# Where eight small fills stand beside the first loads of the expert stage: one-core attention and expert layer

## The chip, the cores and the metric

The kernel runs on one core of one Trainium2 chip. The time is the device time of one execution in microseconds (us); lower is better. The core has five engines that run side by side: TensorE (PE, matrix products; its weight loads are listed as PEld), VectorE (DVE), ScalarE (ACT), GpSimd (POOL) and SyncE (SP, which here only issues DMAs). Each executes its own instructions in order and waits for others by semaphores. DMAs are issued by SP, ACT and POOL.

## The reference

Attention over 8 batches and 8 heads, with 32 global and 512 local positions of head size 64 (local positions see a window of 32 on either side and the global ones). Its output, 4352 rows of 512, goes through a layer of 8 experts, where each row goes to one:

```python
attn_out = _attn_ref(**attn_kwargs)
x = attn_out.transpose(0, 2, 1, 3).reshape(B * S, H * D)
...
expert_idx = np.argmax(logits, axis=1)          # logits: cosine of x and expert_emb, over tau
for e in range(E):
    mask = expert_idx == e
    h = np.maximum(x[mask] @ w1[e], 0.0)         # w1: 512 x 1024
    out[mask] = gate_w[mask, None] * (h @ w2[e]) # w2: 1024 x 512
```

## The kernel before

**Stage one, attention and routing.** For each batch the kernel computes the attention, chooses an expert for each row, and scatters the rows, 128 at a time, by indirect DMAs of POOL (line 838) to a table `xs` in DRAM. In `xs` each expert has a region of `CAP` rows that is filled from its start; a row holds 512 values, the gate and the row's number.

**The fills.** The last block of an expert's rows is seldom full. `fill_rest(e, eng)` (line 1119) writes 128 neutral rows from the tile `fill` behind the last row of expert `e`, at a place that it reads from `runi` (the running counts) by a register load. Expert 0's fill is issued by SP, those of experts 1 to 7 by POOL. Each is a DMA of 257 KB.

**Stage two, the items.** An item is a block of 128 rows of one expert. Two blocks of expert 0 (`EARLY = 2`) are computed early, between the last steps of stage one, by `early_block` (functions in the list `block`, products on line 196 of the profile). The items 0, 1, 2, ... follow. Where item `w` finds its rows and its weights stands in a small table `tab` (`table`, line 1127: some 45 tiny DVE operations, recorded in the list `listed`, and issued by `small`). The first 24 of them stand before the early blocks' last part, the others later. Items 0 and 1 need no table, as their places are known; SP, DVE, ACT and PE read the table by register loads from item 2 on.

One item, in `item` (line 1287):

- `load_x(w)`: four DMAs of 64 KB for the rows (`xr`, line 157) and a small one for the gate and number (`gt`, line 159), all on SP, in 512-byte pieces out of `xs`.
- `turn_x`, `split_x`: DVE turns the rows (`xk`, line 168), ACT and DVE make the two parts of each value, `xH` and `xL` (lines 1246 and 1247), since a product is formed as WH\*xH + WL\*xH + WH\*xL.
- `up(0)`, `up(1)`: 12 products on PE each (line 1315), one half of the hidden vector `h` each. `send_h` rectifies a half on ACT (`relu`, line 1264) and stores it to DRAM (`put_h`: `hd`, line 1272, a DMA of ACT's queue).
- `get_h(w, nh)`: SP loads the half back in a turned order (`hq`, line 1275); `turn_h`, `split_h` make `hk`, `hH`, `hL`.
- `down(0)`, `down(1)`: 12 products each; they stand one item later, between the next item's products (`pend["down"]`). `give` scales by the gate and scatters the rows to the output (POOL, line 176).
- `w_parts`, `slices`: the parts WH (ACT, lines 1210 and 1309) and WL (DVE, lines 1211 and 1310) of the next weights, from the staging tiles `stg`, which `first_w` and `load_w` load on SP.

**What sets the order.** All of this is written in program order per engine (`manual_schedule`): an engine's queue is the order of the calls. On SP, before item 0: the fill of expert 0, `load_x(0)`, `load_x(1)`, four loads of the second expert's first weights (`first_w(0, 0, 4)`, 512 KB each). In item 0: `load_x(2)`, `get_h(0, 0)`, a weight load, `get_h(0, 1)`, a weight load; in item 1: `load_x(3)` and so on. A load of rows by a register's value, as `load_x(2)`, must wait for every DMA that may have written the rows: all scatters and all fills. `load_x(0)` and `load_x(1)` wait for the scatters and expert 0's fill only.

Of the kernel before, what the change touches and what calls it, by code (L numbers as in the profile page):

```python
# [107 lines left out]
def tile_kernel(ctx: ExitStack, tc: tile.TileContext, qk, va, emb, tau, wraw, cst, out):  # L108
    nc = tc.nc
# [160 lines left out]
    with ExitStack() as actx:  # L270
# [41 lines left out]
        ahead = [0]  # L312
# [44 lines left out]
        first = io.tile([P, 4, RS], F32, name="raw")  # L357
# [16 lines left out]
        for n, i in enumerate((0, NBQ - 2)):  # L374
            for q in range(4):
                m = _mask_of(i + q % 2) * P
                rows = slice(32 * q, 32 * q + 32)
# [615 lines left out]
        for g in loads:  # L993
            n = len(loads[g])
# [121 lines left out]

    fills = []

    def fill_rest(e, eng):

        r = eng.value_load(runi[:1, e : e + 1], min_val=e * CAP, max_val=e * CAP + NT)
        ins = eng.dma_start(xs[ds(r, P), :], fill)
        for f in fills + scat + early:
            tc.declare_no_dep(ins.ins, f.ins, reason="disjoint rows")
        fills.append(ins)
# [77 lines left out]
        return tab, nitem  # L1203

    tab = {}

    def first_parts(hf, c):

# [4 lines left out]
    first = [(0, c) for c in (0, 2, 4, 6, 1, 3, 5, 7)] + [(1, c) for c in range(8)]  # L1213

    def slices(n):
        for _ in range(n):
            first_parts(*first.pop(0))
# [10 lines left out]
    def load_x(w):  # L1228
        r = entry(nc.sync, 0, w, NE * CAP)
        return rows_of(xrs[w % 2], gts[w % 5], xs[ds(r, P), :], True)  # L1230

    def load_w(w):
        r = entry(nc.sync, 1, w, 2 * NE - 1)
        src = wraw[ds(r, 1), :, :].rearrange("a p (c n) -> p (a c) n", n=WRUN)
        for n in range(2):
            cs = slice(2 * n, 2 * n + 2)
            new = {"cond": entry(nc.sync, 4 + n, w, 1)}
            nc.sync.dma_start(st0[w % 2][:, cs, :WRUN], src[:, cs, :], **new)
# [13 lines left out]
    def turn_x(w):  # L1252
        turn_blocks(xk, xrs[w % 2])

    def split_x(w):
        parts_of(flat(xHs[w % 2]), flat(xLs[w % 2]), xk)
# [20 lines left out]
    def turn_h(nh):  # L1277
        turn_blocks(hk, hqs[nh])
# [8 lines left out]
    def item(w, pend):  # L1287

        xH, xL = xHs[w % 2], xLs[w % 2]
        rp = entry(nc.tensor, 2, w, 1)  # L1290
        regs = entries(w)
        if w < 2:
            held.append((w, regs))
        reads = []
        made = []
        todo = [(w, regs, c) for c in range(8)]
        if w == 0:
            todo = todo[:4]
        elif w == 1:
            todo = [(*held[0], c) for c in range(4, 8)] + [(*held[1], c) for c in range(4)]  # L1300
        elif w == 2:
            todo = [(*held[1], c) for c in range(4, 8)] + todo

        def w_parts(n):
            for _ in range(min(n, len(todo))):
                v, (ra, rv), c = todo.pop(0)
                cs = slice(c * 512, (c + 1) * 512)
                s3 = cols(st0[v % 2], cs.start, cs.stop).unsqueeze(1)
                a = nc.scalar.copy(WH[c][:, ds(ra, 1)], s3)  # L1309
                b = nc.vector.tensor_tensor(WL[c][:, ds(rv, 1)], s3, WH[c][:, ds(rv, 1)], ALU.subtract)  # L1310
                made.extend([(v, c, a), (v, c, b)])

        def product(o, a, W, hf, start=False, stop=False):
            w3 = W[:, ds(rp, 1), hf * 512 : (hf + 1) * 512]
            return nc.tensor.matmul(o.unsqueeze(1), a, w3, start=start, stop=stop)  # L1315

        def up(nh):
            g = ps_1.tile([P, 512], F32, name="g1")
            for k in range(4):
                c = 2 * k + nh  # L1320
                reads.append(product(g, xH[:, k, :], WH2[c], 0, start=k == 0))
                reads.append(product(g, xH[:, k, :], WL2[c], 0))
                reads.append(product(g, xL[:, k, :], WH2[c], 0, stop=k == 3))
            return g

        out = {}

        def down(nh):
            if nh == 0:
                out["g2"] = g2s[w % 2]  # L1330
            g, ks, made = out["g2"], range(4 * nh, 4 * nh + 4), []
            for k in ks:
                made.append(product(g, hH[:, k, :], WH2[k], 1, start=k == 0))
                made.append(product(g, hH[:, k, :], WL2[k], 1))
            for k in ks:
                made.append(product(g, hL[:, k, :], WH2[k], 1, stop=k == 7))
            return made

        def done():
            give(gts[w % 5], out["g2"], obp.tile([P, DM + 1], F32, name="ob"))  # L1340

        def send_h(nh, g):
            relu(nh, g)
            put_h(w, nh)

        ga = up(0)
        if "done" in pend:
            pend["done"]()
        if w > 2 and w + 1 < NI:
            load_w(w + 1)  # L1350
        if w + 2 < NI:
            load_x(w + 2)
        if w == 0:
            send_h(0, ga)
            slices(3)
            send_h(1, up(1))
            slices(3)
            block[9]()
            block[10]()
            get_h(w, 0)  # L1360
            first_w(1, 0, 1)
            get_h(w, 1)
            first_w(1, 1, 2)
            w_parts(4)
        elif w == 1:
            send_h(0, ga)
            w_parts(2)
            turn_h(0)
            split_h(0)
            gb = up(1)  # L1370
            reads.extend(pend["down"](0))
            send_h(1, gb)
            first_w(1, 2, 3)
            get_h(w, 0)
            first_w(1, 3, 4)
            w_parts(2)
            load_w(w + 1)
            turn_h(1)
            split_h(1)
            turn_x(w + 1)  # L1380
            split_x(w + 1)
            w_parts(4)
            get_h(w, 1)
            reads.extend(pend["down"](1))
        elif w == 2:
            turn_x(w + 1)
            turn_h(0)
            split_x(w + 1)
            split_h(0)
            turn_h(1)  # L1390
            send_h(0, ga)
            w_parts(2)
            split_h(1)
            gb = up(1)
            reads.extend(pend["down"](0))
            send_h(1, gb)
            w_parts(2)
            get_h(w, 0)
            load_w(w + 1)
            w_parts(8)  # L1400
            get_h(w, 1)
            reads.extend(pend["down"](1))
        else:
            if w < NI - 1:
                turn_x(w + 1)
            turn_h(0)
            if w < NI - 1:
                split_x(w + 1)
            w_parts(1)
            split_h(0)  # L1410
            turn_h(1)
            send_h(0, ga)
            w_parts(1)
            split_h(1)
            w_parts(1)
            gb = up(1)
            reads.extend(pend["down"](0))
            send_h(1, gb)
            get_h(w, 0)
            w_parts(8)  # L1420
            get_h(w, 1)
            if w in (8, NSURE - 1):
                nc.gpsimd.drain()
            reads.extend(pend["down"](1))
        for v, c, m in made:
            for r in reads:
                tc.declare_no_dep(m.ins, r.ins, reason="the other slot")
                tc.declare_no_dep(r.ins, m.ins, reason="the other slot")
        for i, (v, c, m) in enumerate(made):
            for u, d, o in last_made + made[:i]:  # L1430
                if c == d and (v - u) % 2:
                    tc.declare_no_dep(m.ins, o.ins, reason="another half")
        last_made[:] = made
        after = {"down": down, "next": done}
        if "next" in pend:
            after["done"] = pend["next"]
        return after
# [12 lines left out]
    with tc.manual_schedule():  # L1450
        nc.vector.tensor_copy(runi, run[:1])
        fill_rest(0, nc.sync)
        load_x(0)
        load_x(1)
        for e in range(1, NE):
            fill_rest(e, nc.gpsimd)
        listed = []
        tab["tab"], nitem = table(listed)

        def small(n):  # L1460
            while listed and n:
                listed.pop(0)()
                n -= 1

        small(24)
        for i, f in enumerate(block[:9]):
            if i:
                f()
            slices((4, 0, 2, 0, 2, 0, 0, 0, 0)[i])
            if i == 8:  # L1470
                first_w(0, 0, 4)
                turn_x(0)
                split_x(0)
                small(len(listed))
                slices(2)
                turn_x(1)
                split_x(1)
        pend = {}
        for w in range(NSURE):
            pend = item(w, pend)  # L1480
# [94 lines left out]
```

## Time and profile before

| what | value |
|---|---|
| runs shown | 699.07 us median of 3 (695.35 to 699.75) |
| profiled execution | 692.65 us |
| its span, first to last instruction | 690.9 us |
| mean granted TensorE clock | 0.977 of full speed |
| PE busy | 635.1 us, 92% of the span |
| fills of POOL | 7, of 257.0 KB each |

The profiled execution is 6.4 us faster than the median of the runs shown; 1.75 us of its time lie outside the span. Times inside the trace count from the span's start. Attention and routing end at about 265 us, and the items run from 270 us to the end.

### The profile page before, as it was taken

Reading aid. Unit: us, or ns where it says so; the run is one execution under the profiler, and the core shown is the slowest. Engines: PE = TensorE matmul, PEld = TensorE weight load, DVE = VectorE, ACT = ScalarE, POOL = GpSimd, SP = SyncE. Lnnn points to the kernel's source line nnn. Section 1 sums busy time; section 2 is a strip of 40 time slices with the busy share of each in tenths; the row PEclk is TensorE's granted clock in tenths of the full one; section 3 lists DMA queues with packets and bytes.
Section 4 is the critical chain, followed back from the end, with each engine's and each line's share of the span. In section 5 each row is a group of like instructions: output and inputs, shape, how many; then the busy total and the mean of one; then the engine's idle time right before and its main releaser. Section 6 shows DMA issues by size and latency. Waiting matters only on the chain.

```text
span 690.9 us, 23126 instructions
## 1 busy us (share of the span) xinstructions
PE 635.1 (92%) x7423; PEld 495.4 (72%) x7425; DVE 525.5 (76%) x1724; ACT 455.6 (66%) x962; POOL 98.6 (14%) x179
## 2 busy tenths in 40 slices
PE   8889888779788897898999999999999999999994
PEld 4667666667576644577888888887787877878883
DVE  2859778698777875797888887887787877878881
ACT  4667758658676433676777677775676757677771
POOL 2011122212213341001011011010101010101101
PEclk9999999999989999999999999999999999999997
DMA  8998889788899538877565587678877779685551
GB/s 271 304 277 249 259 265 280 216 272 285 271 302 279 170 138 259 238 251 221 164 168 150 154 242 206 206 217 263 228 229 229 210 255 261 195 267 162 148 156 36
DMA packets 125207, 154.67 MB, mean 224 GB/s; under 512 B 15945, under 2 KB 81609, under 8 KB 125080
## 3 DMA queue, kind: packets, MB, share of 16 engines
q1 hardware_dynamic: 80744, 114.48, 57.1%
q10 hardware_dynamic: 38016, 18.88, 9.1%
q0 software_dynamic: 6320, 19.71, 7.5%
q8 instruction: 69, 1.13, 0.7%
q14 instruction: 58, 0.48, 0.2%
HBM read 161.36 MB, written 40.94 MB: 293 GB/s over the span
## 4 chain that ended last, share of the span: by engine, by line
PE 52%; DMA 14%; DVE 12%; issue 12%; ACT 6%; SPq 3%; ACTq 1%; DVEq 1%; POOL 0%; POOLq 0%; another core or an unknown queue 0%
PE g L1315 26%; PE po L196 8%; PE pt L199 7%; PE pt L196 5%; PE s_ps L196 5%; DMA xr<-xs 4%; DVE WL L1310 4%; DMA hq<-hd 3%; DMA hd<-h 3%; ACT WH L1309 3%; DVE hk L168 2%; DMA raw<-in_qk_dram 2%; PE g L196 1%; SPq L157 1%; ACT h L1264 1%
## 5 line engine op out<-in xcount | busy, mean ns | idle before, releaser
L1310 DVE TENSOR_TENSOR WL<-stg,WH 128x512 f32 (+1 forms) x288 | 184.4, 683 | 34.3 <-ACT WH L1309 33.6
L1309 ACT CAST WH<-stg 128x512 f32 (+1 forms) x288 | 163.6, 618 | 37.0 <-ACT h L1264 35.5
L1315 PE MATMUL g<-WH,hH 128*128 (+1 forms) x288 | 114.7, 398 | 11.3 <-ACT hH L1246 11.1
L1315 PE MATMUL g<-WH,xH 128*128 (+1 forms) x288 | 113.1, 393 | 3.5 <-ACT xH L1246 3.5
L1315 PE MATMUL g<-WL,hH 128*128 (+1 forms) x288 | 113.4, 394 | 0.0
L1315 PE MATMUL g<-WL,xH 128*128 (+1 forms) x288 | 112.9, 392 | 0.5 <-DVE WL L1310 0.5
L1315 PE MATMUL g<-WH,xL 128*128 (+1 forms) x288 | 113.0, 392 | 0.0
L176 POOL DMA_INDIRECT out_dram<-ob x37 | 36.0, 974 | 387.6 <-DVE xk L168 186.7
L553 ACT ACTIVATE pb<-pb,nm 128x128 f32<-128x128 f32 x256 | 80.0, 395 | 10.3 <-DVE nm L536 10.3
L1315 PE MATMUL g<-WH,hL 128*128 (+1 forms) x288 | 77.9, 393 | 0.0
L1315 PEld LDWEIGHTS g<-WH,hH 128*128 128x128 f32 x288 | 54.9, 190 | 27.6 <-ACT hH L1246 12.3
L168 DVE STREAM_TRANSPOSE hk<-hq 128x512 f32<-128x512 f32 x72 | 50.6, 703 | 24.8 <-DMA hq<-hd 21.1
L1315 PEld LDWEIGHTS g<-WH,xH 128*128 128x128 f32 x288 | 54.5, 189 | 15.8 <-ACT xH L1246 4.3
L1315 PEld LDWEIGHTS g<-WL,xH 128*128 128x128 f32 x288 | 54.3, 189 | 13.0 <-DVE WL L1310 1.5
L1315 PEld LDWEIGHTS g<-WH,hL 128*128 128x128 f32 x288 | 54.6, 190 | 11.5
L1315 PEld LDWEIGHTS g<-WL,hH 128*128 128x128 f32 x288 | 54.8, 190 | 11.2
L1315 PEld LDWEIGHTS g<-WH,xL 128*128 128x128 f32 x288 | 54.5, 189 | 11.6 <-DVE xL L1247 0.4
L1246 ACT CAST hH<-hk 128x512 fp32r<-128x512 f32 x72 | 44.6, 620 | 25.4 <-DVE hk L168 24.8
L196 PE MATMUL s_ps<-raw 64*32 64x128 f32 (+1 forms) x1792 | 46.8, 281 | 11.8 <-issue 10.8
L536 DVE CUSTOM_DVE_ANT_0 pb<-s_ps,mask 128x128 f32<-128x128 f32 x192 | 44.2, 285 | 15.5 <-PE s_ps L196 15.5
L196 PE MATMUL po<-vt,pT 128*32 128x65 f32 x2048 | 46.4, 231 | 10.3 <-issue 10.0
L565 ACT COPY pT<-pt 128x512 f32<-128x512 f32 x64 | 34.6, 588 | 31.7 <-PE pt L199 30.3
(197 smaller groups left out, 880.6 us busy)
## 6 DMA issues: line engine op xcount, KB each, us to landing
stg<-in_wraw_dram SPq DMA_DIRECT2D x70, 1024.0 KB
vt<-in_va_dram SPq DMA_DIRECT2D x96, 260.0 KB
hd<-h ACTq DMA_DIRECT2D x72, 256.0 KB
hq<-hd SPq DMA_DIRECT2D x72, 256.0 KB
raw<-in_qk_dram SPq DMA_DIRECT2D x56, 304.0 KB
xr<-xs SPq DMA_DIRECT2D x152, 64.0 KB
vt<-in_va_dram SPq DMA_DIRECT2D x32, 130.0 KB
stg<-in_wraw_dram SPq DMA_DIRECT2D x16, 256.0 KB
```

The costliest lines, as they stand in the source:

```text
L157: made.append(nc.sync.dma_start(x[32 * g : 32 * g + 32].rearrange("p (t n) -> p t n", n=P), src))
L168: nc.vector.transpose(xT.rearrange("p (k t n) -> p t k n", k=4, t=4), x.rearrange("p (t k n) -> p t k n", t=4, k=4))
L176: nc.gpsimd.indirect_dma_start(out=out[:, :], out_offset=bass.IndirectOffsetOnAxis(ap=ob[:, DM : DM + 1].bitcast(U32), axis=0), in_=ob[:, ...
L196: return counted(nc.tensor.matmul(out, lhsT, rhs, start=start, stop=stop), 4 if lhsT.dtype == F32 else 2)
L199: return counted(nc.tensor.transpose(out, in_, eye), 2)
L536: nc.vector.tensor_tensor_reduce(state["pb", g][grp][:, cs], ps[:, grp, cs], mk, -ISQ, 3.0e38, ALU.add, ALU.min, nm[:, n : n + 1],)
L553: nc.scalar.activation(pb[:, cs], pb[:, cs], AF.Exp, bias=nm[:, n : n + 1], scale=-1.0)
L565: nc.scalar.copy(pT, state["tp", g, grp])
L1246: nc.scalar.copy(tH, x)
L1309: a = nc.scalar.copy(WH[c][:, ds(ra, 1)], s3)
L1310: b = nc.vector.tensor_tensor(WL[c][:, ds(rv, 1)], s3, WH[c][:, ds(rv, 1)], ALU.subtract)
L1315: return nc.tensor.matmul(o.unsqueeze(1), a, w3, start=start, stop=stop)
```

## The change

The seven fills on POOL get a wait: each may start only when the ten DMAs of `load_x(0)` and `load_x(1)` have landed. In item 0 the first half of `h` is rectified and stored (`send_h(0, ga)`) first; `turn_x(1)`, `split_x(1)` and the rest of the table, which stood before item 0, follow it, and two of six `slices` move from before the second half's store to behind it.

```diff
-    def fill_rest(e, eng):
+    def fill_rest(e, eng, behind=()):
 
         r = eng.value_load(runi[:1, e : e + 1], min_val=e * CAP, max_val=e * CAP + NT)
         ins = eng.dma_start(xs[ds(r, P), :], fill)
+        for o in behind:
+            tc.add_manual_dep(
+                ins.ins,
+                o.ins.name,
+                mybir.DependencyInfo(mybir.DependencyClass.Sync, mybir.DependencyReason.DATA),
+                reason="the first rows go ahead",
+            )
...
             load_w(w + 1)
+        if w == 0:
+            send_h(0, ga)
+            turn_x(1)
+            split_x(1)
+            small(len(listed))
         if w + 2 < NI:
             load_x(w + 2)
         if w == 0:
-            send_h(0, ga)
-            slices(3)
+            slices(2)
             send_h(1, up(1))
-            slices(3)
+            slices(4)
...
         fill_rest(0, nc.sync)
-        load_x(0)
-        load_x(1)
+        rows = load_x(0) + load_x(1)
         for e in range(1, NE):
-            fill_rest(e, nc.gpsimd)
+            fill_rest(e, nc.gpsimd, rows)
...
                 turn_x(0)
                 split_x(0)
-                small(len(listed))
                 slices(2)
-                turn_x(1)
-                split_x(1)
```

How the queues stand. On POOL, from the last scatter of rows on; `mask` is the output of the first early block, `DMAHW` are semaphores of DMAs of SP and ACT, `DMASW` of POOL's. Before:

```order
L1121 TENSOR_LOAD runi_74 [waits DVE_49]
L1121 ISA x2
L1122 ISA
L1122 DMA xs_57<-fill_80 128x514 [waits DMASW2_49]
L1121 TENSOR_LOAD runi_74
L1121 ISA x2
L1122 ISA
L1122 DMA xs_57<-fill_80 128x514 [waits DMASW3_49]
L176 DMA out_0_dram<-mask_134 4352x512 [waits DMASW4_49,DVE_49,Activation_49]
```

On POOL, the same place with the change:

```order
L1121 TENSOR_LOAD runi_74 [waits DVE_49]
L1121 ISA x2
L176 DMA out_0_dram<-mask_134 4352x512 [waits DMASW2_49,DVE_49,Activation_49]
L1122 ISA
L1122 DMA xs_57<-fill_80 128x514 [waits DMAHW4_49,DMAHW3_49,DMAHW5_49,DMAHW2_49,DMAHW6_49,DMAHW1_49,DMAHW7_49,DMAHW0_49,DMASW3_49]
L1121 TENSOR_LOAD runi_74
L1121 ISA x2
L1122 ISA
L1122 DMA xs_57<-fill_80 128x514 [waits DMASW4_49]
```

The output of the early block now stands ahead of all fills, and the first fill waits for the loads; the other six follow it in the queue, each behind its own register load.

On SP, `load_x(2)` and what is queued behind it, with the change; the DMASW semaphores of its first DMA are those of the seven fills:

```order
L1239 TENSOR_LOAD tab_5894 [waits DVE_49]
L1239 ISA x2
L1487 TENSOR_LOAD nitem_5895 [waits DVE_49]
L1487 ISA x2
L157 ISA
L157 DMA xr0_5768<-xs_57 32x4x128 [waits DMASW5_49,DMASW4_49,DMASW6_49,DMASW3_49,DMASW7_49,DMASW1_49,DMAHW5_49,DMASW0_49,DVE_49]
L157 ISA
L157 DMA xr0_5768<-xs_57 32x4x128 [waits DMAHW6_49]
```

On SP, the same place before, up to the first load of `h`:

```order
L1226 TENSOR_LOAD tab_5894 [waits DVE_49]
L1226 ISA x2
L157 ISA
L157 DMA xr0_5768<-xs_57 32x4x128 [waits DMASW5_49,DMASW3_49,DMASW6_49,DMASW2_49,DMASW7_49,DMASW1_49,DMAHW4_49,DMASW0_49,DVE_49]
L157 ISA
L157 DMA xr0_5768<-xs_57 32x4x128 [waits DMAHW5_49]
L157 ISA
L157 DMA xr0_5768<-xs_57 32x4x128 [waits DMAHW6_49]
L157 ISA
L157 DMA xr0_5768<-xs_57 32x4x128 [waits DMAHW7_49]
L159 ISA
L159 DMA gt2_5772<-xs_57 128x1x2 [waits DMAHW1_49]
```

SP's order of DMAs is unchanged; a register load of `nitem` (the number of items), which stood far behind, now stands ahead of `load_x(2)`. The wait for the seven fills is there before and after.

On ACT, item 0 before (`xH1` is item 1's, `h` the first half, `hd00` its store):

```order
L1246 CAST xH1_5782<-xk_5775 128x512 [waits DVE_49]
L1264 ACTIVATE h_5787<-g1_6001 128x4x4x32 [waits PE_49,Activation_49]
L1272 DMA hd00_58<-h_5787 128x4x128 [waits DMAHW3_49,Activation_49]
L1210 CAST WH2_5754<-stg1_91 128x512
L1210 CAST WH3_5755<-stg1_91 128x512
```

With the change, its lines' numbers larger by 13, ACT has:

```order
L1277 ACTIVATE h_5787<-g1_5975 128x4x4x32 [waits PE_49,Activation_49]
L1285 DMA hd00_58<-h_5787 128x4x128 [waits DMAHW2_49,Activation_49]
L1259 CAST xH1_5782<-xk_5775 128x512 [waits DVE_49]
L1223 CAST WH2_5754<-stg1_91 128x512
L1223 CAST WH3_5755<-stg1_91 128x512
```

The first half's rectifier and store have moved ahead of item 1's `xH`. PE's order is the same in both.

## Rows read from the trace of the kernel before

**Rows 1.** Page, part 4: share of the span by engine on the chain that ended last.

```profile
PE 52%; DMA 14%; DVE 12%; issue 12%; ACT 6%; SPq 3%; ACTq 1%; DVEq 1%; POOL 0%; POOLq 0%; another core or an unknown queue 0%
```

**Rows 2.** Waits of PE, 260 to 330 us: us in total, times, longest.

```profile
PE g L1315 <- ACT hH L1246: 5.4, 3, 2.3
PE g L1315 <- ACT xH L1246: 3.5, 1, 3.5
```

**Rows 3.** Chain that ended last, 260 to 270 us: start, duration, what.

```profile
262.72 5.24 DMA xr<-xs
...
269.79 0.50 PE g L1315
```

**Rows 4.** DMA queues, 263 to 268 us: packets, MB, share of 16 engines.

```profile
q1 hardware_dynamic: 1163, 0.47, 49.2%
q0 software_dynamic: 220, 0.70, 39.1%
```

**Rows 5.** Chain, other stretches: loads of `xr` and `hq`, issue to landing.

```profile
320.07 4.43 DMA hq<-hd
...
495.35 3.99 DMA xr<-xs
...
598.02 2.57 DMA hq<-hd
```

**Rows 6.** Stretches: length, busy of PE, PEld, DVE, ACT, POOL, granted clock, DMA share, GB/s.

```profile
265.00:270.00 5.00, 1.53 (x5) 0.46 (x4) 0.94 (x2) 1.16 (x3) 0.00 (x0) 1.00 0.84 209
270.00:275.00 5.00, 5.00 (x15) 3.68 (x15) 4.52 (x26) 0.78 (x2) 0.00 (x0) 0.66 0.90 333
...
285.00:290.00 5.00, 2.70 (x12) 1.91 (x11) 2.93 (x5) 2.86 (x6) 0.00 (x0) 1.00 1.05 265
```

**Rows 7.** Timeline of PE, 264 to 296 us: start, duration, instruction, idle before.

```profile
288.52 0.50 PE L1315 MATMUL g<-WH,hH 128*128 128x512 f32 x1 [2.30 <-ACT hH L1246]
...
292.67 0.50 PE L1315 MATMUL g<-WH,hH 128*128 128x512 f32 x1 [1.10 <-ACT hH L1246]
```

**Rows 8.** Timeline of POOL, 250 to 300 us.

```profile
256.86 1.17 POOL L1122 DMA_DIRECT2D xs<-fill  x2
...
262.22 0.54 POOL L1122 DMA_DIRECT2D xs<-fill  x1 [0.90 <-issue]
263.63 0.54 POOL L1122 DMA_DIRECT2D xs<-fill  x1 [0.87 <-issue]
283.40 1.01 POOL L176 DMA_INDIRECT out_dram<-ob  x1 [19.23 <-ACT WH L1309]
```

**Rows 9.** DMA issues, 245 to 300 us: count, KB each, median us to landing.

```profile
xs<-fill POOLq DMA_DIRECT2D x7, 257.0 KB, 4.8
```

**Rows 10.** Timeline of SP, 251 to 300 us.

```profile
266.55 0.57 SPq L159 DMA_DIRECT2D gt<-xs  x1
...
275.52 2.15 SPq L157 DMA_DIRECT2D xr<-xs  x4
277.86 0.66 SPq L159 DMA_DIRECT2D gt<-xs  x1
279.66 0.36 SPq L1275 DMA_DIRECT2D hq<-hd  x1
```

**Rows 11.** Timeline of ACT and DVE in items 0 and 1.

```profile
273.74 0.17 DVE L1134 CAST tab<-tabf 128x6 int32<-128x6 f32 x1
...
276.33 0.59 ACT L1264 ACTIVATE h<-g 128x512 f32<-128x512 f32 x1
...
287.11 0.70 DVE L168 STREAM_TRANSPOSE hk<-hq 128x512 f32<-128x512 f32 x1
...
293.26 0.70 DVE L168 STREAM_TRANSPOSE xk<-xr 128x512 f32<-128x512 f32 x1
```

**Rows 12.** DMA queue of SP, 268 to 275 us: packets, MB, share of 16 engines.

```profile
q1 hardware_dynamic: 801, 2.07, 87.3%
```

More of the change, by code (lines that the diff above doesn't have):

```diff
@@ L1205, in tile_kernel, with small @@
     tab = {}
+    listed = []
+    def small(n):
+        while listed and n:
+            listed.pop(0)()
+            n -= 1
     def first_parts(hf, c):
@@ L1452, in tile_kernel @@
         fill_rest(0, nc.sync)
-        load_x(0)
-        load_x(1)
+        rows = load_x(0) + load_x(1)
         for e in range(1, NE):
-            fill_rest(e, nc.gpsimd)
-        listed = []
+            fill_rest(e, nc.gpsimd, rows)
         tab["tab"], nitem = table(listed)
[L1460 to L1463, printed above, removed]
         small(24)
```

## The prediction, made before the changed kernel was run

> **What bounds the kernel now.** I read first the chain that ended last, by engine, to see whether one engine is the limit. PE holds 52% of it, DMAs 14%, DVE 12% and ACT 6% [rows 1]: over most of the kernel PE is the limit, and the other shares come from places where PE waits. The change touches one of these, so I read PE's waits from 260 to 330 us. There are few: one of 3.5 us for item 0's `xH`, and three for `hH`, 5.4 us together [rows 2]. At the first, the chain shows why: the last load of item 0's x goes out at 262.72, takes 5.24 us and lands at 267.96, and PE starts item 0 at 269.79, 1.83 us after that [rows 3]. While that load is under way, two queues share the DMA engines: SP's with 49.2% and POOL's with 39.1% of their time, and POOL's 0.70 MB are fills [rows 4]. Elsewhere a load of `xr` has taken 3.99 us, and one of `hq` 2.57 [rows 5]. After the wait PE's granted clock is 0.66 of full speed from 270 to 275 us [rows 6], between its two levels of 1.2 and 2.4 GHz; in those 5.00 us it loses 5.00 x 0.34 = 1.7 us against full speed.
>
> The next place is the first `down(0)`. PE ends item 1's products at 288.52 - 2.30 = 286.22, waits 2.30 us for `hH`, and 1.10 more ahead of `down(1)` at 292.67 [rows 7]. So what PE gains early only counts if `down(0)` of item 0, at 288.52, comes earlier too. This decides the case: what comes ahead of `down(0)` on the other engines must gain as well.
>
> **The change part by part.**
>
> *Item 0's x without the fills.* The fills no longer go out ahead of x0. Its landing then lies between 5.24 us (nothing gained: its own 512-byte pieces set it) and 2.57 us, the quickest load out of DRAM in [rows 5]. I take 2.57, since the one thing known to share those microseconds, POOL's queue, is gone. x0 lands at 262.72 + 2.57 = 265.3, PE starts at 265.3 + 1.83 = 267.1, and gains 2.7 us. The wait ahead of it shrinks from 3.5 to 0.8 us, and with so short a wait I expect no fall of the clock: the wait of 2.30 us ahead of 288.52 left it at 1.00 from 285 to 290 us [rows 6, 7]. That gives the 1.7 us as well: 4.4 us together. Item 1's products would end at 286.22 - 4.4 = 281.8.
>
> *The fills.* POOL now waits for the last of the ten loads, item 1's gate and number, issued at 266.55 [rows 10]. With 2.57 us, the first fill can go at 269.1. The other six stand behind it, each with its register load in between. Fills that were not held up went out 263.63 - 262.22 = 1.41 us apart; two in a row with their registers ready take 1.17 us, or 0.59 each [rows 8]. I take 1.41, as the order shows a register load ahead of each fill: the last one goes out at 269.1 + 6 x 1.41 = 277.6 (by 0.59, 272.6). A fill took 4.8 us to land [rows 9], with x0 and x1 beside it. Now it has four weight loads, 2.07 MB at 87.3% of the engines [rows 12], beside it, so I keep 4.8: the last lands at 282.4, or at 277.4 by the quicker pitch. Behind the fills on POOL stands the output of the second early block, at 283.40 [rows 8], which comes after 277.6 + 0.5 anyway. The early block's first output goes out a little earlier, and no one reads it.
>
> A rule of the Trainium skill speaks for an earlier landing. Its page "DMA: Bandwidth & Descriptors" (section "Anatomy of one DMA — SWDGE (gpsimd) path") gives a DMA of POOL a fixed part of some 2.0 us and then 436 GB/s: 2.6 us for 257 KB, an estimate by that page against the row's 4.8. By it the last fill would land at 280.2 and the sum below would be -0.7 in place of +1.5, or 698.4. The page's figure is for one DMA alone, which the row is not, so the row stays.
>
> *What waits for the fills.* SP's first DMA of `load_x(2)` waits for all seven; it did so before as well, but then they had landed long before 275.52, where the table let it go (its last operation ends at 273.91 [rows 10, 11]). Now the table comes later: it stands behind item 0's first half on DVE. By how much I bound from rows: relu0 was at 276.33 [rows 11] and would be some 4 us earlier with item 0, the table's rest ran up to 273.91 with DVE busy 4.52 of 5 us [rows 6], so it ends at about 276 and SP's register loads, one more of them (`nitem`), at about 278. That is earlier than 282.4 and costs nothing while the fills are later; by the quicker pitch it costs up to 1 us.
> So `load_x(2)` goes at 282.4 in place of 275.52. On SP everything behind it waits: its own five DMAs (275.52 to 278.52, 3.0 us [rows 10]), then `get_h(0, 0)`, a weight load, `get_h(0, 1)`. `get_h(0, 0)` went at 279.66 and now goes at 285.4. Between 2.57 and 4.43 us [rows 5] for its landing I take 2.57, as the fills are then done: 288.0. From DVE's turn of `hk` at 287.11 to PE at 288.52 are 1.41 us [rows 7, 11], so `down(0)` starts at 289.4: 0.9 us later than before. The stores of `h` go ahead 4 us, and gain nothing, for SP is not there to read them.
>
> *PE's wait moved.* PE now waits from 281.8 to 289.4, 7.6 us in one piece where it had 2.30. The wait of 3.5 us was followed by a clock of 0.66, so I expect the same loss, 1.7 us, over `down(0)` and what follows; 1.10 of it lie where PE waited ahead of `down(1)` anyway. Cost: 0.6 us, between 0 (the wait of 2.30 cost nothing) and 1.7.
>
> *The rest.* Item 2's x lands some 7 us later, at about 285.4, and DVE turns it at 293.26 [rows 11]. The `slices` moved behind the second half run on ACT and DVE beside PE's long wait. `xH` of item 1 stands behind relu0 on ACT, but PE reads it only after item 0's second half. All three at nothing; their cover is PE's work on item 0 and the wait ahead of `down(0)`.
>
> *Sum.* -4.4 early, given back whole; +0.9 for `down(0)`, +0.6 for the clock: +1.5 us. The profiled execution's 692.65 would be 694.15. It lies 6.4 us under the median, and the same difference on the median is 699.07 + 1.5 = 700.6.
>
> **The rivals.**
>
> *The early gain survives.* If the fills go 0.59 us apart, they have landed at 277.4, `get_h(0, 0)` goes at 280.4 and lands at 283.0, `down(0)` starts at 284.4, 4.1 us earlier, after a wait of 2.6 us like that of before, without loss of clock: 695.0. For it speaks that registers could be loaded while the first fill waits, and that the page's landing is shorter; against it that only the first fill's registers stand ahead of the wait. At most the 1.10 us ahead of `down(1)` go as well: 693.9.
>
> *The fills land later still: slower.* Each us by which the last fill lands after 280.9 makes the kernel a us slower, for PE's whole wait there hangs on it. Fills of 7 x 0.257 = 1.80 MB and weights of 2.07 MB now want the engines together. At 209 GB/s, the rate of 265 to 270 us with the same kinds of traffic [rows 6], 3.87 MB from 267.1 on take 18.5 us, to 285.6: 3.2 us beyond my 282.4, so +4.7, or 703.8. For it: 87.3% of the engines are taken by weights until 275 us. Against it: at 333 GB/s [rows 6] the same is done at 278.7. The skill's same page, section "Issuing engines are not separate DMA queues", says that queues of different issuers share the 16 engines, and the drawn-out x0 of [rows 3, 4] agrees.
>
> *It does not do what it says.* If x0's 5.24 us come of its small pieces, or of x1's loads behind it, item 0 starts at 269.8 as before, the clock falls as before, item 1's products end at 286.2 and only a wait of 3 us stands ahead of `down(0)`. Then -4.4 and +0.6 drop out, +0.9 stays, and a later x1 adds up to its own lateness, some 1 us: 700 to 701, near my number by another way.
>
> **How the numbers follow.** My forecast, 700.6 with a range of its own of 699 to 702.5: 0.50. The gain survives, 695.0: 0.26. The fills land later, 703.8: 0.16. It does not do what it says, 700.5: 0.08. The range reaches from 694.0, the end of the gain, to 704.5: it leaves out the later half of the third case and a part of the second, and runs that scatter as before's (695.35 to 699.75). About 1%, 7 us, is what a measurement of this kernel can tell from no change, so faster begins under 692.1, which not even the second case reaches, and slower over 706.1, which the third reaches only if the last fill lands after 287: 0.05 each.
>
> **What would show it.** In the changed profile: x0's last load lands in under 4 us, PE's wait for `xH` is under 1.5 us and the clock of 270 to 275 is 1.00 (first step); POOL's fills begin at about 269 and end at about 278, 1.4 us apart (second); SP's `load_x(2)` goes at about 282, its wait put down to a fill, and `get_h(0, 0)` right behind it, not behind the store (third); PE's largest wait of the stage is that ahead of the first `down(0)`, some 7 us, with a clock under 0.8 in the 5 us behind it (fourth). The prediction is wrong if the last fill lands before 280 or after 284, or if what follows `down(0)` soaks up its shift: the third wait for `hH` is 5.4 - 2.30 - 1.10 = 2.0 us long [rows 2], and a later start could shorten it.

## The result, and the profile after

The changed kernel takes 700.83 us (median of 20 runs, 694.89 to 706.22), the kernel before 696.22 us on the same chip (20 runs, 686.41 to 709.88): a ratio of 1.0127 with a 95% interval of 1.0091 to 1.0163. The ratio compares the fast runs of each kernel, while the medians of all runs lie 4.6 us, or 0.7%, apart, and the profiled executions of e2, f3 and g1 further down are among their kernels' slow runs. The forecast of 700.6 was near the measured time, but that was luck: it stood for a step of 1.5 us from 699.07, the median of three runs, and the twenty have a median 2.85 us under that. The step itself is three times the forecast's by the medians (4.6 us), and six times by the ratio (1.27% of 699 us are 8.9). The profiled execution takes 699.77 us with a span of 698.1.

The places where the time goes are read from the changed kernel's trace in the order of [rows 2 to 12]. PE's waits from 260 to 330 us first (us in total, times, longest):

```profile
PE g L1328 <- ACT hH L1259: 12.3, 2, 8.2
```

The wait for `xH` of [rows 2] is gone, and the waits for `hH` have grown from 5.4 to 12.3 us. The timeline of PE puts one ahead of the first `down(0)` and one ahead of the second half of item 1's `h`:

```profile
289.28 0.79 PE L1328 MATMUL g<-WH,hH 128*128 128x512 f32 x1 [8.15 <-ACT hH L1259]
...
309.06 0.50 PE L1328 MATMUL g<-WH,hH 128*128 128x512 f32 x1 [4.20 <-ACT hH L1259]
```

The stretches (columns as in [rows 6]) show the gain in front, and the price behind it:

```profile
270.00:275.00 5.00, 5.00 (x17) 3.01 (x16) 3.29 (x21) 4.10 (x9) 1.86 (x4) 1.00 1.01 349
275.00:280.00 5.00, 5.00 (x22) 3.92 (x21) 4.93 (x13) 3.21 (x6) 0.60 (x2) 1.00 1.06 297
280.00:285.00 5.00, 1.13 (x5) 0.59 (x4) 2.83 (x5) 1.74 (x3) 2.45 (x1) 1.00 0.47 130
285.00:290.00 5.00, 0.72 (x2) 0.63 (x3) 1.40 (x2) 1.12 (x2) 0.00 (x0) 0.61 0.81 240
290.00:295.00 5.00, 5.00 (x18) 3.95 (x17) 3.23 (x5) 1.97 (x4) 0.00 (x0) 0.71 0.96 299
```

From 270 to 280 PE has full speed (1.00, the level of 2.4 GHz) and no gap; then it does almost nothing for 8 us and comes back with clocks of 0.61 and 0.71. The DMA engines are full from 270 to 280, with shares of 1.01 and 1.06.

POOL's timeline has the fills, which before were all issued by 264.2 us [rows 8]:

```profile
267.31 0.60 POOL L1122 DMA_DIRECT2D xs<-fill  x1 [8.81 <-DMA gt<-xs]
...
275.30 0.54 POOL L1122 DMA_DIRECT2D xs<-fill  x1 [0.92 <-issue]
279.94 2.51 POOL L176 DMA_INDIRECT out_dram<-ob  x1 [4.11 <-DVE WL L1323]
```

In the DMA queues of 270 to 281 us (columns as in [rows 4]) POOL's, that is the fills, takes half of the 16 engines:

```profile
q0 software_dynamic: 558, 1.84, 49.3%
```

SP's timeline shows what is held behind them:

```profile
282.39 1.94 SPq L157 DMA_DIRECT2D xr<-xs  x4
284.53 0.66 SPq L159 DMA_DIRECT2D gt<-xs  x1
285.30 0.37 SPq L1288 DMA_DIRECT2D hq<-hd  x1
...
293.71 0.35 SPq L1288 DMA_DIRECT2D hq<-hd  x1
294.82 0.34 SPq L1256 DMA_DIRECT2D stg<-in_wraw_dram  x1
296.95 1.48 SPq L1251 DMA_DIRECT2D stg<-in_wraw_dram  x2
298.53 0.34 SPq L1288 DMA_DIRECT2D hq<-hd  x1
```

`load_x(2)` goes at 282.39 where it went at 275.52 [rows 10], and `get_h(0, 0)` right behind it. SP has read the table and stands at the semaphores of `load_x(2)` from 277.8 us; its waits of 265 to 300 us (us in total, times, longest) put this down to the fills:

```profile
SPq L157 <- DMA xs<-fill: 4.3, 2, 3.1
```

Further on the two 1 MB loads of `load_w(2)` (line 1251) go at 296.95, and `get_h(1, 1)` 1.58 us behind them. In the kernel before the same three stood apart, as its timeline of SP shows:

```profile
292.03 1.49 SPq L1238 DMA_DIRECT2D stg<-in_wraw_dram  x2
296.11 0.34 SPq L1275 DMA_DIRECT2D hq<-hd  x1
```

The chain that ended last (start, duration, what) names the two long transfers of the changed kernel, a store of `h` and that load:

```profile
270.21 10.08 DMA hd<-h
...
298.53 9.02 DMA hq<-hd
```

**How far each place is shifted.** Stage one does not end at the same microsecond in every execution. So I count from the rectifier of the second early block, on ACT at 262.49 us before and at 262.85 in the changed kernel. Against it, as worked out from the timelines, item 0's first rectifier comes 7.1 us earlier than before, item 1's first 4.2 earlier, the first `down(0)` 0.4 later, the first half of item 2's 0.4 later, the second half of item 2's 6.2 later; at item 4's first half 3.7 us are left, since the kernel before has its own wait for `hH` there (PE's 2.0 us at 326) and the changed one has none, and item 6 starts 3.5 us late. From there to 535 us the shift stays between 2.7 and 4.3 us. Later waits differ from execution to execution: of those over 1 us this one has 1.29 us at 484, 1.25 at 573, 2.36 at 632 and 4.02 at 686, that of before only 3.54 at 677, and the last rectifier of all comes 7.6 us late. So 3.5 us are lost by item 6, beside 4.6 us between the medians.

### The profile page after: what moved, and what is told of

Its sections match the earlier page's. It is cut to its first block, busy times and chain, and to the rows that moved or that the text cites. A ratio compares the mean times of both kernels' runs of the same rounds, so it can differ in the third digit from the quotient of the medians.

```text
span 698.1 us, 23134 instructions
## 1 busy us (share of the span) xinstructions
PE 629.7 (90%) x7425; PEld 493.4 (71%) x7425; DVE 524.8 (75%) x1724; ACT 455.7 (65%) x962; POOL 100.4 (14%) x179
## 4 chain that ended last, share of the span: by engine, by line
PE 56%; DMA 17%; DVE 9%; issue 9%; ACT 5%; SPq 2%; ACTq 1%; DVEq 0%; POOL 0%; POOLq 0%; another core or an unknown queue 0%
PE g L1328 31%; PE pt L199 7%; PE po L196 7%; DMA hd<-h 6%; PE pt L196 5%; DMA hq<-hd 5%; PE s_ps L196 5%; DVE WL L1323 2%; DMA raw<-in_qk_dram 2%; ACT WH L1322 2%; DMA xr<-xs 2%; PE g L196 1%; ACT h L1277 1%; DVE hk L168 1%; DMA stg<-in_wraw_dram 1%
## 5 line engine op out<-in xcount | busy, mean ns | idle before, releaser
L176 POOL DMA_INDIRECT out_dram<-ob x37 | 37.5, 1015 | 381.5 <-DVE xk L168 165.7
L168 DVE STREAM_TRANSPOSE hk<-hq 128x512 f32<-128x512 f32 x72 | 50.7, 704 | 28.8 <-DMA hq<-hd 24.5
L1260 DVE TENSOR_TENSOR hL<-hk,hH 128x512 fp32r<-128x512 f32 x72 | 49.5, 687 | 4.6 <-ACT hH L1259 2.8
```

Source lines behind the costliest of these rows:

```text
L168: nc.vector.transpose(xT.rearrange("p (k t n) -> p t k n", k=4, t=4), x.rearrange("p (t k n) -> p t k n", t=4, k=4))
L176: nc.gpsimd.indirect_dma_start(out=out[:, :], out_offset=bass.IndirectOffsetOnAxis(ap=ob[:, DM : DM + 1].bitcast(U32), axis=0), in_=ob[:, ...
L1260: nc.vector.tensor_tensor(tL, x, tH, ALU.subtract)
```

## The experiments

Theory A: the late fills hold `load_x(2)` on SP until 282 us, and everything behind it in SP's queue is late with it; in a second step the late weight loads of `load_w(2)` come to stand right ahead of `get_h(1, 1)`. The rivals: B, item 0's new order and not the fills; C, chance late in the kernel. "Shift" is that of item 6's first rectifier (346.98 us before), counted from the early block as above; the `down(0)` column is counted so too. Each kernel has runs of before on its own chip beside it (the second number). "Profiled" is the time of the one execution that the last four columns are read from; that of before took 692.65.

| kernel | median, before | ratio (95%) | profiled | load_x(2) at | get_h(0, 0) at | first down(0) | shift |
|---|---|---|---|---|---|---|---|
| changed | 700.83, 696.22 | 1.0127 (1.0091 to 1.0163) | 699.77 | 282.39 | 285.30 | +0.4 | +3.5 |
| e1_wait_only | 696.06, 691.37 | 1.0082 (1.0017 to 1.0146) | 695.54 | 278.89 | 281.80 | -1.6 | -0.2 |
| e2_order_only | 697.24, 691.37 | 1.0044 (1.0006 to 1.0083) | 704.79 | 286.91 | 290.01 | +0.9 | +6.1 |
| e3_w2_later | 696.61, 691.37 | 1.0084 (1.0049 to 1.0120) | 694.94 | 282.17 | 285.07 | -0.7 | +1.6 |
| e4_both_later | 693.09, 691.37 | 0.9983 (0.9942 to 1.0024) | 689.48 | 284.57 | 280.54 | -4.8 | -2.5 |
| f1_x0_wait | 698.81, 691.38 | 1.0120 (1.0075 to 1.0165) | 695.01 | 279.19 | 282.09 | -1.5 | +0.7 |
| f2_before_w2 | 695.11, 691.38 | 1.0054 (1.0008 to 1.0099) | 697.02 | 274.27 | 278.27 | -1.3 | +0.2 |
| f3_wait_both | 695.10, 691.38 | 1.0044 (0.9995 to 1.0093) | 698.00 | 284.80 | 281.14 | -4.0 | -0.3 |
| f4_x2_later | 691.77, 691.38 | 1.0038 (0.9994 to 1.0082) | 695.83 | 286.89 | 282.82 | -4.1 | -0.5 |
| g1_late_fills | 699.20, 691.33 | 1.0110 (1.0060 to 1.0160) | 710.78 | 290.52 | 293.42 | +3.3 | +8.3 |
| g2_x0_both | 692.38, 691.33 | 1.0040 (0.9997 to 1.0083) | 689.93 | 284.09 | 280.05 | -4.7 | -2.1 |
| g3_x0_both_w | 693.89, 691.33 | 1.0052 (1.0012 to 1.0091) | 693.65 | 280.58 | 276.12 | -4.8 | -0.7 |
| h1_change_again | 698.80, 693.82 | 1.0066 (1.0031 to 1.0101) | 703.98 | 283.20 | 286.10 | +0.6 | +5.0 |

The early block's rectifier stands at 262.49 before, at 262.85 in the changed kernel, and in the order of the other rows at 261.27, 267.53, 263.88, 263.79, 262.02, 262.58, 264.31, 266.44, 268.14, 263.04, 260.25 and 263.52.

**The two halves of the change alone.** e1 is the kernel before with the fills' wait (`fill_rest` as in the change):

```diff
-        load_x(0)
-        load_x(1)
+        rows = load_x(0) + load_x(1)
         for e in range(1, NE):
-            fill_rest(e, nc.gpsimd)
+            fill_rest(e, nc.gpsimd, rows)
```

> The kernel before, with only the fills' wait for x of items 0 and 1. Theory A (SP's load of item 2's x is held until about 282 us by the late fills, and everything behind it on SP is late with it): the fills go out at 267 to 275 us, load_x(2) at about 282, the first down(0) at about 289, and a second wait of PE for the second half of item 1's h of 3 to 5 us at about 309: as the changed kernel, 3 to 6 us slower than before. Rival B (the new order of item 0 and the table behind it cost the time): within 1.5 us of before, or faster by up to 4. Rival C (the difference comes from waits for DMAs late in the kernel that vary from run to run): load_x(2) and down(0) late as in A, but both kernels within 1 us of before at 345 us.

e2 is the changed kernel without it:

```diff
         for e in range(1, NE):
-            fill_rest(e, nc.gpsimd, rows)
+            fill_rest(e, nc.gpsimd)
```

> The changed kernel without the fills' wait: only item 0's new order. Theory A: x0 lands late as before (PE starts item 0 at about 270), the fills have landed by 268, but the table now stands behind item 0's first half, at about 277 to 281 us, so load_x(2) goes at 279 to 282.5 and down(0) at 286 to 289.5; what follows is as late as SP is: between 0 and 6 us slower than before. If only the fills count (rival B reversed): load_x(2) by 277 and the time within 1 us of before. Rival C: no difference at 345 us.

Neither half is harmless. In e1 the table is ready at 268.58 and the last fill, issued at 273.54, lets `load_x(2)` go at 278.89. In e2 the fills are out by 268.92, but item 0's x comes beside them again, item 0 starts at 274.51, and the table behind its first half is ready late, as DVE's timeline shows:

```profile
285.12 0.17 DVE L1141 CAST tab<-tabf 128x6 int32<-128x6 f32 x1
```

The register loads follow, and `load_x(2)` goes at 286.91, which is 281.9 counted as before's times (the early block is 5.0 us later here). Both put the first `down(0)` some 7 us behind `load_x(2)`, as theory A has it. Rival B in its strict form falls by the time, since the wait alone has a ratio above 1; e1's shift would fit it. A's size for e1 was missed: `down(0)` came 1.6 us early and not as late as in the changed kernel (+0.4), and the shift was -0.2 against the expected 3 to 6 us. Rival C is not excluded by e1, whose medians differ by 4.7 us all the same.

**Dose.** f1 lets the fills wait for item 0's loads only, g1 lets them wait for the four weight loads too (there `first_w` also returns its DMAs):

```diff
-        rows = load_x(0) + load_x(1)
+        rows = load_x(0)
+        load_x(1)
```

```diff
-        for e in range(1, NE):
-            fill_rest(e, nc.gpsimd, rows)
...
-                first_w(0, 0, 4)
+                rows += first_w(0, 0, 4)
+                for e in range(1, NE):
+                    fill_rest(e, nc.gpsimd, rows)
```

> The changed kernel, but the fills wait only for item 0's five loads, not for item 1's. All times against the end of the early block on ACT (the rectifier at 262.5 us of before). Theory A: the fills begin some 2.5 us earlier, the last one lands 1 to 2.5 us earlier (280 to 281), load_x(2) goes with it, no earlier than the table lets it (277.7), and the first down(0) is at 287 to 288 in place of 289; item 0 starts as early as in the changed kernel (at most 0.5 us later). Total 0 to 3 us faster than the changed kernel. Rival B (the order alone sets it): down(0) as in the changed kernel within 0.5 us. Rival F (fills beside x1 and the first half of x0 take the gain in front): item 0 starts 1 us or more later.

> The changed kernel, but the fills wait for the four weight loads (2 MB) of SP too. Times against the early block's end, as shifts from before. Theory A with a dose: load_x(2) goes with the last fill, and each us by which it is later makes the first down(0) a us later. Fills begin at about 272 instead of 267, go out 1.2 us apart and land in 3 to 5 us without the weights beside them: load_x(2) at 283 to 285, first down(0) at +1 to +3 (changed kernel +0.4; with the wait for x0 alone -1.5), wait of PE 9 to 11 us. Rival G (the DMA engines' total, not the fills' start, sets the landing): load_x(2) and down(0) as in the changed kernel within 0.5 us.

Counted from the early block, `load_x(2)` goes at 279.65 in f1 (279.19 + 0.46), 280.10 in e1, 280.78 in e3, 281.87 in e2, 282.03 in the changed kernel and 284.87 in g1, and the first `down(0)` follows 7.4, 6.8, 7.1, 7.6, 6.9 and 7.0 us behind it: over a range of 5.2 us each us of `load_x(2)` is about one us of `down(0)`, whether the fills or the table hold it. Counted so, f1's last fill went out 3.1 us earlier than the changed kernel's (271.80 against 274.94), and let SP go 2.4 us earlier. In g1 they began at 279.37, later than I had put them (272 us):

```profile
279.37 0.60 POOL L1122 DMA_DIRECT2D xs<-fill  x1 [15.58 <-DMA hd<-h]
```

The profile puts this wait down to a store of `h`, but the semaphores say otherwise: POOL's long wait, from 270.7 to 278.4, ends with the fourth weight load, issued at 271.82 and landed at 278.41. Rival G falls. In time f1's expected gain over the changed kernel does not show: its median is 7.4 us over before.

**The second step.** e3 puts `load_w(2)` behind `get_h(1, 1)`; f2 does the same to the kernel before:

```diff
-            load_w(w + 1)
             turn_h(1)
             split_h(1)
             turn_x(w + 1)
             split_x(w + 1)
             w_parts(4)
             get_h(w, 1)
+            load_w(w + 1)
```

> The changed kernel, with the two 1 MB weight loads of item 1 (load_w(2)) put behind get_h(1, 1) on SP. Theory A with its second step (those 2 MB, now issued right ahead of get_h(1, 1), draw out its landing from 2.4 to 9 us): the first down(0) stays at about 289.3, get_h(1, 1) lands within 4 us of its issue, the wait of 4.2 us at 309 goes or falls under 1 us, and the kernel is 2 to 4 us faster than the changed one, within 2 us of before. Rival D (h's store or SP being late by itself makes that wait): the wait stays at 3 us or more and the time stays with the changed kernel. Rival C: no difference.

> The kernel before, with only the two 1 MB loads of load_w(2) put behind get_h(1, 1) on SP. Theory A, second step: before had get_h(1, 1) 2.7 us behind the weights, waiting for the store of h, and that store took 7 us beside them; without them the store lands in 3 to 5 us, get_h(1, 1) lands 2 to 4 us earlier, but PE did not wait there, so the time stays within 2 us of before; the weights come 3 to 4 us later and may make PE wait once at 316 to 326. Rival: a gain of over 3 us.

In e3 the wait at 309 us is gone: between the halves of item 2's `h` the shift goes from -0.6 to -0.5 us, where it jumps from +0.4 to +6.2 in the changed kernel. Two smaller waits come later (2.16 us at 316, 1.76 at 329), and the net is 2.0 us by item 6, of which 1.1 were there at the first `down(0)` already. So the 2 MB ahead of that load made the second wait. The other kernels bear it out: wherever `load_x(2)` is held and the 2 MB go right ahead of `get_h(1, 1)`, the shift jumps between those halves, by 5.7 us in the changed kernel, 4.2 in its repeat h1, 3.9 in e1, 4.5 in e2, 4.7 in f1 and 4.7 in g1; with the 2 MB behind it, by 0.1 in e3 and 0.0 in f2. In h1 that wait is 2.46 us long (308.37), after a first one of 8.37, and the shift is +5.0:

> The changed kernel once more, for how far its places repeat. Theory A: load_x(2) 280.5 to 283 against the early block's end, first down(0) some 7 us behind it (between -1 and +1.5 us of before), the second wait, for the second half of item 1's h at about 309, again 2 to 5 us, shift at 345 us +1.5 to +4.5. Rival C (chance): no second wait, or a shift under +1 us. Time: 3 to 8 us over before.

In time the move shows nothing: e3's median is 5.2 us over before, the changed kernel's 4.6 and 5.0. f2 has two waits of 1.5 us at 314 and 327 us, where one was expected, and its median is 3.7 us over before, more than the 2 us expected.

**Taking SP's queue out of it.** f4 moves `load_x(2)` behind `get_h(0, 1)`, e4 makes both moves, f3 makes both on e1:

```diff
-        if w + 2 < NI:
+        if 0 < w < NI - 2:
             load_x(w + 2)
...
             get_h(w, 1)
             first_w(1, 1, 2)
+            load_x(w + 2)
```

> The changed kernel with only load_x(2) moved behind get_h(0, 1) on SP. Theory A: the first down(0) 4 to 5 us earlier than before, as in the kernel with both moves, but load_w(2) stands again right ahead of get_h(1, 1), whose landing takes 7 to 10 us, and PE waits 3 us or more for it at about 300 to 307: shift at 345 us between -1 and +3 us, 2 us or more worse than with both moves. Rival D (the 2 MB have nothing to do with it): shift as with both moves, -2 to -3.

> As the one before, and load_x(2) stands behind get_h(0, 1) and its weight load on SP too, so that neither the fills nor the table hold back get_h(0, 0). Theory A: get_h(0, 0) goes at about 275, the first down(0) at 284.5 to 285.5 (then held by the parts of weights on DVE), no second wait over 1 us, and the kernel is 2 to 5 us faster than before, 6 to 9 faster than the changed one. Rival E (item 2's x, now loaded at 282 to 285, is late next): PE waits for xH of item 2 at about 292 and the gain falls under 1 us. Rival C: no difference at 345 us.

> The kernel before with the fills' wait, item 0's old order (table early), and both SP moves (load_x(2) behind get_h(0, 1), load_w(2) behind get_h(1, 1)). Theory A: as the kernel with both moves and the new order, the first down(0) 4 to 5 us earlier than before against the early block's end, PE's second wait at about 293 of 2 to 4 us, no third over 2 us; shift at 345 us -2 to -4 us, the time 1 to 4 us under before. If the old order is worse with the fills late (h's store, behind xH of item 1, lands later): shift 0 to -2.

In all three the first `down(0)` comes 4.0 to 4.8 us earlier than before: the gain in front is real, and SP's queue had taken it. It is kept for one product group only. e4's PE waits again, ahead of `down(1)`:

```profile
293.12 0.80 PE L1328 MATMUL g<-WH,hH 128*128 128x512 f32 x1 [3.47 <-ACT hH L1259]
```

and its chain shows why:

```profile
284.57 4.79 DMA xr<-xs
289.44 0.37 ACTq L1285
289.84 0.63 ACT WH L1322
290.50 0.55 DVE WL L1323
...
291.79 0.63 DVE hk L168
292.44 0.63 ACT hH L1259
```

Item 2's x now goes out in its turn on SP, which does not wait for a fill there. ACT's store of `h` (line 1285), ready since 285.5, waits on that load until 289.44; the parts of weights and `hk` stand behind it. Nor did `get_h(0, 0)` go at 275, as I had expected: it went at 280.54, when `h`'s store, issued at 271.2, had landed. Theory A missed f4's second wait: `get_h(1, 1)` took 6.4 us there (298.45 to DVE's turn at 304.86), but PE, 2.59 us late at 295.49 already, did not wait for it. By median f4 is 0.4 us over before, e4 1.7 and f3 3.7, where I had expected e4 and f3 to be faster; none of the three can be told from before by its ratio. f4 differs from the changed kernel in one move, that of `load_x(2)`, and its ratio is 1.0038 against 1.0127, and 1.0066 in the repeat, whose interval overlaps f4's.

**Shorter traffic beside it.** g2 is e4 with f1's wait, g3 also puts the fourth 512 KB weight load behind `get_h(0, 1)`:

```diff
-                first_w(0, 0, 4)
+                first_w(0, 0, 3)
...
             get_h(w, 1)
+            first_w(0, 3, 4)
             first_w(1, 1, 2)
```

> The changed kernel with the fills waiting only for item 0's x, load_x(2) behind get_h(0, 1) and load_w(2) behind get_h(1, 1). Theory A and its third step (the store of h is drawn out beside fills and weights): h's store lands 1 to 2 us earlier than in the kernel with both moves and the full wait, the first down(0) at -5 to -6, but PE waits again ahead of down(1) for 2 to 4 us; shift at 345 us -2 to -4, the time 1 to 4 us under before. If the sum of the DMAs' bytes sets it: as with the full wait, -2.5.

> As the one before, and the fourth of the four 512 KB weight loads stands behind get_h(0, 1) too, so that 2.07 MB become 1.55 MB beside the fills and the stores of h. If bytes set the landing of h's store: 1.5 us earlier again (0.5 MB at 330 GB/s), first down(0) at -5.5 to -7, limited at -7 by item 0's own start; shift at 345 us 0.5 to 1.5 us better than the one before. If not: no change, or the weight load that comes late makes PE wait at 290 to 300.

Neither improves on e4: the first `down(0)` stays at -4.7 and -4.8, and PE waits 5.57 us (g2) and 2.84 us (g3) ahead of `down(1)`. In g3 `get_h(0, 0)` goes 0.9 us earlier than in e4, counted from the early block, but six parts of weights keep DVE until 280.2 and its turn of `hk` stands behind them. No version beats the kernel before. By the medians, the five kernels whose `load_x(2)` was moved stand 0.4 to 3.7 us over before, and those in which the fills or the table hold it 4.6 to 7.9.

## Why the prediction was wrong

*Item 0's x.* Right. The last of the four loads goes out at 261.33 and has landed at 263.29, in 1.96 us (forecast 2.57). The loads also go out 1.3 us earlier, which the forecast did not have: the last scatter, for which SP waits there, lands sooner without fills beside it (SP's wait ends at 259.9, before at 261.2). PE starts item 0 at 266.21 without a wait (forecast 267.1, 0.8 us of wait), and the clock of 270 to 275 us is 1.00 in place of 0.66.

*The fills.* Right in sum: begun at 267.31 (269.1), 1.33 us apart on average (1.41), and `load_x(2)` let go at 282.39 (282.4). Two errors of some 2 us cancel in that sum: the last fill went out 2.3 us early (275.30 for 277.6), and the fills took 6.9 to 8.1 us to land, not 4.8. The rival with quick fills fell: the last one was issued at 275.30 and SP went on 7.1 us later, with the DMA engines full. In g1, where the weights had landed first, the seven took 2.6 to 3.2 us each. The estimate of 2.6 us for one fill, from the page "DMA: Bandwidth & Descriptors" of the Trainium skill (section "Anatomy of one DMA — SWDGE (gpsimd) path"), is near g1's and far from the changed kernel's. The same page of the Trainium skill says, in its section "Issuing engines are not separate DMA queues", that DMAs of all issuers run on the same 16 engines. The trace agrees: from 270 to 281 us the queues of POOL, SP and ACT hold 49.3%, 28.8% and 19.2% of them.

*SP's queue.* Right: `get_h(0, 0)` at 285.30 (285.4), the first `down(0)` at 289.28 (289.4), after 8.15 us of wait (7.6). The early gain was given back whole here.

*The clock.* It fell, to 0.61 and 0.71, but cost nothing on the end: the shift is +0.4 at `down(0)` and still +0.4 at item 2's first half. The wait of 1.10 ahead of `down(1)` took it, so the 0.6 us of the sum were 0 here.

*The step that failed* is the one headed "The rest", with the sum made from it: it followed SP's delay only as far as `get_h(0, 0)` and costed nothing behind it. I had written that `get_h(0, 0)`, a weight load and `get_h(0, 1)` wait, and did not go on to `load_w(2)`, which moved from 292.03 to 296.95, up to `get_h(1, 1)`. That load then took 9.0 us, PE waited 4.20 us and came back with a clock of 0.66 (310 to 315 us). Together this made 5.7 us, of which 2.4 are given back at item 4, at the third wait for `hH` that the forecast's last sign names; so the forecast's +0.9 at `down(0)` was +0.4, and +1.5 by item 6 was +3.5 (+5.0 in the repeat). e3, where that wait goes, shows the cause of the wait. It does not show that the wait makes the measured step, since e3's time is no better.

*The rivals.* The forecast's "fills land later still" named the right direction with the wrong mechanism: the fills landed when forecast. That the new order costs by itself was not among the rivals, and e2 shows it: the table behind item 0's first half puts `load_x(2)` at the same place without any wait of the fills, though there item 0 is late too. In the changed kernel the table ended at 275.42 (I had put 276) and SP stood ready for `load_x(2)` at 277.8 (278), so this cost some 2 us against before's 275.52 and lay under the fills. Of item 0's six `slices` one moved behind the second half's store, not two, as the section on the change has it; no reading here hangs on it.

*What stays open.* Medians of e1, f1 and f2 lie 3.7 to 7.4 us over before while their shifts by item 6 are -0.2 to +0.7. That leaves 3.5 to 6.8 us that the profiles do not place. After item 6 every profile has waits for `hH`, at other items in each. From 345 us on they sum to 5.7 us in before, 5.6 to 7.9 in the five kernels whose `load_x(2)` was moved, and 6.8 (e3) to 11.2 (g1) in those where it is held, with 10.1 in the changed kernel and 10.9 in its repeat; f2 has 8.7. So part of the step seems to lie there, and no run shows what would tie these waits to the first items; with one profile for each kernel it is not settled.

## What to carry to other kernels

A transfer that is only put off must land before someone needs it, and here its waiter stood in SP's queue ahead of everything that PE needed next; so follow the queue behind a held DMA to the end of the delay, not to its first victim. Two DMAs that meet in a new order can cost more than the delay that made them meet: the first `down(0)` came 0.4 us late, and 2 MB right ahead of a 256 KB load, which then took 9.0 us, added 5.7, of which 2.4 came back. And 1.8 MB moved from a place where PE had other work to one where a result must go to DRAM and back drew that store out to 10.08 us.

## What the runs showed that was not expected

The store of `h` beside fills and weights took 10.08 us by the chain, where before `get_h(0, 0)` could go 2.7 us after the store was issued (276.96 to 279.66). The fills, more than the weights, draw it out: in g1 the store goes out at 275.52 beside the last weights, with the fills still held, and has landed by 279.1. In e4 a store on ACT waited some 4 us on a load of SP, which reads other data: in the trace both DMAs signal by the same semaphore, and the store, ready at 285.5, waits for it until 289.38, when the first of the load's DMAs has landed. In g3 the same store waits 3.5 us, until 285.01, for a weight load that signals by the same semaphore.
